# Largest magnitudes across the partitions: a transpose, a vector maximum and a small matmul in place of GpSimd's partition reduce

## The chip, the cores and the metric

The kernel runs on one core of one Trainium2 chip. Its metric is the device time of one execution in microseconds (us). The engines are named as the profile names them: PE is TensorE's matmul, PEld its weight load, DVE is VectorE, ACT is ScalarE, POOL is GpSimd, SP is SyncE, whose queue issues nearly all DMAs here.

## The reference

Eight batches, each of eight heads, with 512 tokens and 32 state rows of 64 values. Every head does an attention both ways between its tokens and its state; the two results are joined, and a feed-forward layer with layer norm and a residual follows.

```python
scores = scale * x @ state.T ;  a = softmax(scores) ;  xread = a @ state
scores2 = scale * state @ x.T ; a2 = softmax(scores2) ; sread = a2 @ x
y = concat([xread, sread], axis=2)        # 8 batches x 544 rows x 512 after joining the heads
xn = (y - mean) / sqrt(var + 1e-6) * g_ln
out = y + max(xn @ w_ch1, 0) @ w_ch2      # 512 -> 2048 -> 512
```

The inputs are float32, the two weights arrive as float64 words.

## The kernel before

TensorE multiplies in float16. Each operand is split in two float16 halves (a rounded value and its remainder), and a product takes three of the four terms. For that, every operand is first scaled by a power of two, which is taken from its largest magnitude. The largest magnitude is needed on every partition alike: first DVE and ACT find it within each partition, and then `partition_all_reduce` on POOL takes the maximum over the 128 partitions and writes it to all of them. This happens in 16 places:

- once for each of the eight batches, in `attention(b)`: `am` (tile x_am, two columns, one for x and one for the state) goes through the reduce in L172 into tile x_m; L173 and `scales` (L130 to L132) make x_s and x_i of it, and then L180, L181, L188 and L189 make the float16 halves of state and x, which DMAs transpose for the scores (L203);
- once for each of the four units of both weights, in `weight_scale` (L413), from tile w_am to w_m; L415 to L419 make the scale w_s of it.

A unit of a weight goes through `convert`: two raw pieces of 1 MB come in by DMA (L460, L507), ACT takes signs (L437, tile sgn) and magnitudes (L405), DVE their maximum and the float32 bits (L406 to L408), then comes the scale, ACT scales (L443), POOL gives the sign back (L444), ACT rounds to float16 (L451), and POOL makes the remainder (L452).

The first batch is computed while the weights come in. `PLAN` gives the order in which the generators of attention of batches 0 and 1 (a0, a1), the units of the first weight (w0 to w3) and of the second (v0 to v3), and the two products of batch 0 (m: L541, evicted by L544 and L545; n: L602, evicted by L654) are traced. From there the tile framework's planner orders the instructions of each engine, by its own model of their durations, and sets all waits; each engine then runs its queue in order. Batch 1 takes the plain first product too (L541), while `weight_sums` (L480 to L487) makes the other pieces of the first weight. Batches 2 to 7 and the state's rows take the first product by Strassen's scheme in seven products a unit (L560), on four accumulators p1 to p4, which ACT and DVE read (L568 to L594, with one addition on POOL, L586), and the second product in L602, evicted by L619. The attention of batch b+1 is traced between the products of batch b, and its layer norm ends in `normalise` (L322 to L372, the power on POOL in L327), whose pieces go through a transposing DMA into tile xnT.

PSUM has eight banks: `ps_f` gives six single banks to `accumulator()` and `ps_a` one pair to `banks()`. The float32 identity `idf` lies in a buffer of the tag "quad" and is read once, for `fold`.

Of the kernel before, what the change touches and what calls it, by code (L numbers as in the profile page):

```python
# [8 lines left out]
F32 = mybir.dt.float32  # L9
# [3 lines left out]
U32 = mybir.dt.uint32  # L13
# [6 lines left out]
TINY = 1e-30  # L20
F64_MIN = 2.0**-15     # the upper word, read as a float32, of the float64 2**-127
F64_AMAX = 2.0**-12    # the same of 2**-103
SX = 2.0**14   # x and state are scaled so that their largest magnitude lies in [SX, 2 SX)
SE = 2.0**12   # softmax numerators in (0, 1] are scaled by this
SN = 4.0       # normalised activations
SG = 2.0**-1
SW1 = 2.0**3
SW2 = 2.0**13

# Operands are split in two float16 halves, and a product takes three of the four terms.  # L30
A_PIECE = (0, 5, 4, 1, 6, 2, 3)   # where the weight's pieces lie, in the order of the products
# The order of the work on the first batch: attention of batches 0 and 1, the two weights by units,
# the two products.
PLAN = (("a0", 8), ("w0", 3), ("a0", 1), ("w1", 5), ("a0", 5), ("v0", 2), ("w1", 3), ("w2", 2), ("w0", 1),
# [13 lines left out]
def moe_attention(ctx: ExitStack, tc: tile.TileContext, x, state, g_ln, w1, w2, out):  # L48
    """The first product of the feed-forward layer goes by Strassen's scheme in Winograd's form:
    the weight in quarters A (features x inputs), the activations in quarters B (inputs x tokens),  # L50
    seven products of their sums and differences."""
    nc = tc.nc
# [4 lines left out]
    P = 128  # L57
    C = S // P           # token chunks of a batch
    G = H // 4           # groups of four heads
    U = DF // 512        # units of four feature tiles, two of each half  # L60
    QK = 1.0 / float(D) ** 0.5
# [3 lines left out]
    small = ctx.enter_context(tc.tile_pool(name="small", bufs=2))  # L65
    ps_f = ctx.enter_context(tc.tile_pool(name="ps_f", bufs=6, space=PSUM))
    ps_a = ctx.enter_context(tc.tile_pool(name="ps_a", bufs=1, space=PSUM))

    def block(kb, tag, bufs, name):
        """kb kilobytes per partition, out of the buffers that go by that tag."""  # L70
        return main.tile([P, kb * 256], F32, name=name, tag=tag, bufs=bufs)
# [27 lines left out]

    # ---- loads that come first  # L100
    def load_batch(b):
# [15 lines left out]

    idf = quad("idf")[:, 0:P]
    make_identity(nc, idf)
# [5 lines left out]
    def scales(m, c, name):  # L125
        """m [P, n], the same on every partition -> with e the power of two at or below each,
        e / c and c / e."""
        n = m.shape[1]
        inv, s = column(small, name + "_i", n), column(small, name + "_s", n)
        nc.vector.tensor_scalar(inv.bitcast(I32), m.bitcast(I32), EXP_MASK, None, ALU.bitwise_and)  # L130
        nc.vector.tensor_scalar(inv, inv, 1.0 / c, None, ALU.mult)
        nc.vector.reciprocal(s, inv)  # L132
        return s, inv

    def absmax(a, t):
        nc.vector.tensor_reduce(a, t, AX.X, ALU.max, apply_absolute_value=True)

    # ---- gain, the same on every partition
    isg = column(main, "isg")
# [6 lines left out]

    # ---- state operands of a batch
    sh = main.tile([P, G, 2, 2, D], F16, name="sh")
# [5 lines left out]
    def attention(b):  # L154
# [16 lines left out]
        m = column(small, "x_m", 2)  # L171
        nc.gpsimd.partition_all_reduce(m, am, P, bass_isa.ReduceOp.max)  # L172
        nc.vector.tensor_scalar_max(m, m, TINY)  # L173
        sc, isc = scales(m, SX, "x")
# [3 lines left out]
        yield  # L178
        # halves of x and of the state side by side, and transposed: (half, d) on the partitions
        nc.scalar.activation(sh[:, :, 0], sj.unsqueeze(2).broadcast_to([P, G, 2, D]), AF.Copy, scale=sst)  # L180
# [16 lines left out]
        yield  # L197
        # scores, (head, state row) on the partitions
        ps = banks()
# [17 lines left out]
        yield  # L217
        # softmax over the tokens: the state's read
        eb = halves("eb").rearrange("p (i g t) -> p i g t", i=2, g=G)
# [9 lines left out]
        yield  # L229
        # softmax over the state rows  # L230
        ts3 = ts.rearrange("p (k n) -> p k n", n=32)
# [38 lines left out]
        if b > 0:  # L270
            # every head's halves of the numerators, twice, down the partitions
            ek = rows("ek").bitcast(F16).rearrange("p (g j t) -> p g j t", g=G, j=4)
            for i in range(2):
                for j in range(4):
                    nc.sync.dma_start(out=ek[32 * i:32 * i + 32, :, j], in_=ea[32 * j:32 * j + 32, i])  # L275
            nc.sync.dma_start(out=ek[64:128], in_=ek[0:64])
# [16 lines left out]
        else:  # L293
            # nothing else is on the tensor engine yet: a bank for every fourth head
            for j in range(4):
# [18 lines left out]
    def normalise(xr, cw, plain):  # L314
        """Layer norm of two halves of cw chunks of rows; the quarters and their sums in halves,
        transposed."""
        w = cw * 256
# [73 lines left out]

    # ---- weights
    def narrow(u, name):
# [6 lines left out]
    def magnitudes(raw, t, most):  # L400
        """float64 words [P, n, 2] -> in t [P, n] float32 of the same magnitude but of either sign,
        and the largest of the upper words read as float32, whose order is that of the float64."""
        ti = t.bitcast(U32)
        low = raw[:, :, 0].bitcast(U32)
        nc.scalar.activation(t, raw[:, :, 1].bitcast(F32), AF.Abs)  # L405
        nc.vector.tensor_scalar(t, t, F64_MIN, F64_AMAX, ALU.max, ALU.max, accum_out=most)  # L406
        nc.vector.tensor_scalar(ti, ti, 7 << 27, 3, ALU.bitwise_xor, ALU.logical_shift_left)
        nc.vector.scalar_tensor_tensor(ti, low, 29, ti, ALU.logical_shift_right, ALU.bitwise_or)  # L408

    def weight_scale(most, c, name):  # L410
        """Largest upper words [P, 2] -> scales, the same on every partition."""
        m = column(small, name + "_m", 2)
        nc.gpsimd.partition_all_reduce(m, most, P, bass_isa.ReduceOp.max)  # L413
        mi = m.bitcast(U32)
        nc.vector.tensor_scalar(mi, mi, 1 << 27, 4, ALU.bitwise_xor, ALU.logical_shift_left)  # L415
        nc.vector.tensor_scalar(mi, mi, 1, EXP_MASK, ALU.logical_shift_right, ALU.bitwise_and)
        inv, s = column(small, name + "_i"), column(small, name + "_s")
        nc.vector.tensor_scalar(inv, m[:, 0:1], m[:, 1:2], 1.0 / c, ALU.max, ALU.mult)
        nc.vector.reciprocal(s, inv)  # L419
        return s, inv  # L420
# [4 lines left out]
    def convert(u, src, spaces, ts, scale, back, target, engine):  # L425
        """Unit u of a weight, as two times [P, 1024] float64 words, in halves of float16."""
        am = column(small, "w_am", 2)
# [27 lines left out]
    def weights1(u):  # L455
        def src(fh, raw):
            f0 = 2 * (fh * (DF // 2) + u * 256)
            # the first unit's words go ahead of the transposes that the scores wait for, the others not
            with tc.issue_after(marks[0].ins) if u > 0 else nullcontext():
                nc.sync.dma_start(out=raw.rearrange("p (k f) -> p k f", k=4),  # L460
                                  in_=w1[:, f0:f0 + 512].rearrange("(k p) f -> p k f", p=P))
# [11 lines left out]
    def weight_sums(u):  # L473
        """The other four pieces of the first weight, from the halves of its quarters."""
        w = w1c[u].rearrange("p m i k f -> p m i (k f)")
# [45 lines left out]
    def common_scale():  # L521
        """The units of the second weight scaled alike, so that one accumulation takes them all."""
        nc.vector.tensor_reduce(uo, uoq, AX.X, ALU.max)
# [7 lines left out]

    # ---- feed-forward layer
    def first_product_plain(u, xT, cw, hids):
        """Unit u of the hidden layer from the quarters themselves."""
        w = cw * P
# [14 lines left out]
    def first_product(u, xT, cw, hids):  # L550
        """Unit u of the hidden layer, two halves of 128 cw tokens, by Strassen's scheme."""
        w = cw * P
# [89 lines left out]

    # ---- the first batch, while the weights come in
    def first_products():
# [15 lines left out]
    for u in range(U):  # L660
        gens[f"w{u}"] = weights1(u)
        gens[f"v{u}"] = weights2(u, spaces[u])
    # each engine's newest instruction of the first attention: the weights' work keeps behind it
    newest = {}
# [59 lines left out]
```

## Time and profile before

| | us |
|---|---|
| median of 3 runs | 898.94 |
| lowest and highest run | 895.89, 899.03 |
| span of the profiled execution | 896.3 |
| PE busy | 739.4 (82%) |
| DVE busy | 520.0 (58%) |
| ACT busy | 328.9 (37%) |
| POOL busy | 216.7 (24%) |

The profile is of one execution. Its span goes from the first to the last instruction; the page gives no other time for that execution, and its span lies 2.6 us below the median of the runs. Engines work side by side, so their busy times add to more than the span, and a busy time says nothing of when an engine was needed. The idle time in front of a group of instructions, and what ended it, says who waited for whom. Ends of matmuls are modelled, and the spans of POOL's own instructions are rough.

### The profile page before, as it was taken

The page shows a single profiled execution, that of the slowest core. Times are in us where ns is not written, and L with a number is a line of the kernel's source. Part 1 is how long each engine was busy: PE and PEld are TensorE (multiplying, and loading weights), DVE is VectorE, ACT ScalarE, POOL GpSimd, SP SyncE. Part 2 cuts the span into 40 slices and gives each one's busy share as a digit, 9 for nine tenths or more (in the row PEclk, how much of TensorE's full clock was granted, in tenths as well). Part 3 has the DMA queues.
Part 4 walks back from the last instruction along what each step waited for, and adds up shares of the span by engine and source line. Part 5 has one row for each costly group of instructions (what it writes and reads, how often), then busy time and mean ns, then how long its engine had stood idle before and what let it go on. Part 6 is the DMA issues. An engine that isn't in the chain of part 4 may idle for free.

```text
span 896.3 us, 12756 instructions
## 1 busy us (share of the span) xinstructions
PE 739.4 (82%) x5136; PEld 447.1 (50%) x5136; DVE 520.0 (58%) x881; ACT 328.9 (37%) x534; POOL 216.7 (24%) x153
## 2 busy tenths in 40 slices
PE   0120535789699799999999999999999999899997
PEld 0020212334234346864785487458745764685493
DVE  5857336847856546755584578357836674472050
ACT  4555343442434324423542354144415342251030
POOL 0147124641838411112011212021201121020010
PEclk9999957988989899999999999999999999999999
DMA  9950515133050238033802551264145322602000
GB/s 221 308 154 0 141 31 119 24 99 104 11 122 18 52 105 158 5 74 88 157 15 61 129 116 24 75 134 87 30 123 116 48 49 61 118 2 42 24 26 23
DMA packets 146586, 73.83 MB, mean 82 GB/s; under 512 B 125472, under 2 KB 137248, under 8 KB 146080
## 3 DMA queue, kind: packets, MB, share of 16 engines
q1 hardware_dynamic: 146384, 72.77, 34.9%
q8 instruction: 40, 0.66, 0.3%
q10 hardware_dynamic: 144, 0.26, 0.1%
q14 instruction: 18, 0.15, 0.1%
HBM read 28.57 MB, written 9.44 MB: 42 GB/s over the span
## 4 chain that ended last, share of the span: by engine, by line
PE 39%; DVE 17%; issue 13%; DMA 11%; POOL 9%; ACT 8%; SPq 3%; DVEq 0%; ACTq 0%; POOLq 0%
PE acc L560 20%; PE acc L602 17%; DMA xnT<-pc 4%; DMA x_f<-in_x_dram 3%; POOL w_t L444 3%; DVE pc L372 2%; POOL sums L480 2%; DMA s_r<-in_state_dram 1%; SPq L275 1%; POOL w2h L452 1%; POOL w1c L452 1%; DVE pc L348 1%; DVE tq L365 1%; ACT x L188 1%; DVE hid L569 1%
## 5 line engine op out<-in xcount | busy, mean ns | idle before, releaser
L602 PE MATMUL acc<-w2h,hid 128*128 128x512 f16 x1632 | 370.4, 386 | 35.6 <-ACT hid L544 15.1
L602 PEld LDWEIGHTS <-hid 128*128 128x128 f16 x1632 | 160.1, 99 | 229.8 <-issue 18.4
L560 PE MATMUL acc<-xnT,w1c 128*128 128x256 f16 (+1 forms) x2352 | 243.7, 265 | 8.9 <-DMA xnT<-pc 7.2
L560 PEld LDWEIGHTS <-w1c 128*128 128x128 f16 x2352 | 214.7, 98 | 39.9 <-issue 11.2
L541 PE MATMUL acc<-xnT,w1c 128*128 128x512 f16 x384 | 93.6, 407 | 46.3 <-DMA xnT<-pc 46.3
L541 PEld LDWEIGHTS <-w1c 128*128 128x128 f16 x384 | 39.7, 104 | 98.0 <-issue 43.7
L586 POOL TENSOR_TENSOR m<-u,m 128x512 f32<-128x512 f32 (+1 forms) x28 | 33.4, 1191 | 205.3 <-DVE u L585 196.0
L322 DVE BATCH_NORM_STATS2 s<-xr 128x6 f32<-128x512 f32 x32 | 20.6, 685 | 64.5 <-ACT xr L291 64.5
L291 ACT ACTIVATE xr<-banks,ux 128x1024 f32<-128x1024 f32 x14 | 15.6, 1114 | 108.5 <-PE banks L289 107.4
L327 POOL TENSOR_TENSOR rs<-rs,mhalf 128x4 f32<-128x4 f32 (+1 forms) x9 | 12.7, 1407 | 171.4 <-DVE rs L326 144.7
L568 ACT ACTIVATE hid<-u 128x512 f16<-128x512 f32 (+1 forms) x56 | 33.2, 594 | 50.9 <-DVE u L589 50.5
L619 DVE SCALAR_TENSOR_TENSOR xr<-acc,uo,xr 128x512 f32<-128x512 f32 x28 | 20.9, 745 | 51.6 <-PE acc L602 51.3
L444 POOL TENSOR_TENSOR w_t<-w_t,sgn 128x1024 f32<-128x1024 f32 x16 | 35.8, 2255 | 40.8 <-issue 21.8
L569 DVE SCALAR_TENSOR_TENSOR hid<-u,hid 128x512 f16<-128x512 f32 (+1 forms) x56 | 41.9, 750 | 0.0
L372 DVE TENSOR_TENSOR pc<-xn,pc 128x512 f16<-128x512 f32 (+1 forms) x28 | 23.5, 877 | 28.9 <-ACT pc L371 28.9
L569 DVE SCALAR_TENSOR_TENSOR hid<-acc,hid 128x512 f16<-128x512 f32 (+1 forms) x28 | 18.1, 648 | 31.8 <-ACT hid L568 31.7
L248 PE MATMUL banks<-ebT,x 128*128 128x64 f16 x256 | 10.3, 205 | 25.8 <-ACT w_t L443 16.8
L443 ACT ACTIVATE w_t<-w_t,w_s 128x1024 f32<-128x1024 f32 x16 | 17.5, 1140 | 38.5 <-DVE w_s L419 22.8
L203 PE MATMUL banks<-xT,sT 128*32 128x512 f16 x128 | 12.0, 428 | 22.2 <-DMA xT<-x 22.2
L568 ACT ACTIVATE hid<-m 128x512 f16<-128x512 f32 (+1 forms) x28 | 16.6, 593 | 36.1 <-POOL m L586 36.1
L573 ACT ACTIVATE m<-acc 128x512 f32<-128x512 f32 (+1 forms) x28 | 15.5, 552 | 38.3 <-PE acc L560 38.3
L371 ACT ACTIVATE pc<-xn 128x512 f16<-128x512 f32 (+1 forms) x28 | 15.1, 588 | 36.9 <-DMA xnT<-pc 36.8
(120 smaller groups left out, 869.9 us busy)
## 6 DMA issues: line engine op xcount, KB each, us to landing
raw<-in_moe_w_ch_dram SPq DMA_DIRECT2D x16, 1024.0 KB, 5.7
x_f<-in_x_dram SPq DMA_DIRECT2D x16, 512.0 KB, 5.8
out_dram<-xr SPq DMA_DIRECT2D x16, 512.0 KB, 3.2
ek<-ea SPq DMA_DIRECT2D x56, 64.0 KB, 2.0
ek<-ek SPq DMA_DIRECT2D x7, 512.0 KB, 4.2
s_r<-in_state_dram SPq DMA_DIRECT2D x32, 64.0 KB, 5.0
s_j<-in_state_dram SPq DMA_DIRECT2D x8, 64.0 KB, 3.1
sread_rows<-sread SPq DMA_DIRECT2D x32, 16.0 KB, 3.1
```

Of the source, the lines that this page charges most:

```text
L322: nc.vector.bn_stats(s6, xr[t][:, c])
L372: nc.vector.tensor_tensor(pc[:, q, 1], v, pc[:, q, 0], ALU.subtract)
L444: nc.gpsimd.tensor_tensor(t, t, sgn[:, fh], ALU.mult)
L452: engine.tensor_tensor(lo, t, hi, ALU.subtract)
L480: nc.gpsimd.tensor_tensor(o, a, b, ALU.add)
L541: nc.tensor.matmul(ps, lhsT=w1c[u][:, q // 2 * 2 + k // 2, i, k % 2, q % 2 * P:(q % 2 + 1) * P], rhs=xT[:, k // 2 * 2:k // 2 * 2 + 2, j, k ...
L560: nc.tensor.matmul(ps[:, f * w:(f + 1) * w], lhsT=w1c[u][:, A_PIECE[m], i, k, f * P:(f + 1) * P], rhs=xT[:, m, j, k * w:(k + 1) * w], star ...
L568: nc.scalar.activation(hi, v, AF.Relu)
L569: nc.vector.scalar_tensor_tensor(lo, v, 0.0, hi, ALU.max, ALU.subtract)
L586: nc.gpsimd.tensor_tensor(m5, u3, m5, ALU.add)
L602: nc.tensor.matmul(po, lhsT=hid[:, i, q, c * P:(c + 1) * P], rhs=w2h[u][:, j, q], start=first and q == 0 and n == 0, stop=last and q == 3 ...
L619: nc.vector.scalar_tensor_tensor(v, po, uo, v, ALU.mult, ALU.add)
```

## The change

The partition reduce on POOL is replaced in both places by a new function `across`. It transposes the columns of largest magnitudes (two columns on 128 partitions) on PE into PSUM, so that each becomes a row on one partition; DVE takes the maximum of each row (2x128); and a second matmul, with that maximum repeated 128 times as its weight and a corner of the identity as its moving operand, writes the two maxima to all 128 partitions. DVE's next instruction reads them from PSUM. The bank for this comes from a new pool `ps_x`, and `ps_f` has five banks in place of six. The identity gets a tile of its own, since it is now needed throughout. The diff also takes out comments, which are left out here.

```diff
-from concourse import bass_isa, mybir
+from concourse import mybir
...
-    ps_f = ctx.enter_context(tc.tile_pool(name="ps_f", bufs=6, space=PSUM))
+    ps_f = ctx.enter_context(tc.tile_pool(name="ps_f", bufs=5, space=PSUM))
     ps_a = ctx.enter_context(tc.tile_pool(name="ps_a", bufs=1, space=PSUM))
+    ps_x = ctx.enter_context(tc.tile_pool(name="ps_x", bufs=1, space=PSUM))
...
-    idf = quad("idf")[:, 0:P]
+    idf = main.tile([P, P], F32, name="idf")
     make_identity(nc, idf)
...
+    def across(a, name):
+        n = a.shape[1]
+        ps = ps_x.tile([P, 512], F32, name="spread")
+        nc.tensor.transpose(ps[0:n, 0:P], a, idf)
+        top = column(small, name + "_t")
+        nc.vector.tensor_reduce(top[0:n], ps[0:n, 0:P], AX.X, ALU.max)
+        nc.tensor.matmul(ps[:, P:P + n], lhsT=top[0:n].broadcast_to([n, P]), rhs=idf[0:n, 0:n], start=True, stop=True)
+        return ps[:, P:P + n]
...
         m = column(small, "x_m", 2)
-        nc.gpsimd.partition_all_reduce(m, am, P, bass_isa.ReduceOp.max)
-        nc.vector.tensor_scalar_max(m, m, TINY)
+        nc.vector.tensor_scalar_max(m, across(am, "x"), TINY)
...
         m = column(small, name + "_m", 2)
-        nc.gpsimd.partition_all_reduce(m, most, P, bass_isa.ReduceOp.max)
         mi = m.bitcast(U32)
-        nc.vector.tensor_scalar(mi, mi, 1 << 27, 4, ALU.bitwise_xor, ALU.logical_shift_left)
+        nc.vector.tensor_scalar(mi, across(most, name).bitcast(U32), 1 << 27, 4, ALU.bitwise_xor, ALU.logical_shift_left)
```

## The prediction

> **What bounds the kernel now.** I read the page's first two parts, then the same span cut by stage, then the chain of work that ended last, then GpSimd's instructions in order of time, and last the waits.
>
> Page, parts 1 and 2: busy time of three engines, then tenths of 40 slices (22.4 us each).
> ```profile
> span 896.3 us, 12756 instructions
> PE 739.4 (82%) x5136; PEld 447.1 (50%) x5136; DVE 520.0 (58%) x881; ACT 328.9 (37%) x534; POOL 216.7 (24%) x153
> PE   0120535789699799999999999999999999899997
> PEclk9999957988989899999999999999999999999999
> ```
> 82% is an average over two unlike stages: from slice 15 on PE is full at full clock, before it PE is half empty and its clock is down. The same by stage (columns: stretch, its length, busy PE, PEld, DVE, ACT, POOL with instructions, granted clock, DMA share, GB/s):
> ```profile
> 0.00:95.00 95.00, 10.39 (x152) 8.36 (x153) 64.75 (x122) 48.83 (x63) 31.50 (x25) 1.00 0.61 168
> 95.00:260.00 165.00, 115.90 (x515) 48.45 (x515) 97.59 (x158) 61.85 (x85) 69.25 (x41) 0.82 0.30 79
> 260.00:328.00 68.00, 62.00 (x347) 29.35 (x346) 41.35 (x69) 25.19 (x43) 31.85 (x23) 0.95 0.22 44
> 328.00:755.00 427.00, 416.96 (x3093) 274.20 (x3091) 262.77 (x440) 160.36 (x275) 69.47 (x50) 1.00 0.40 85
> ```
> After 328 us, PE is busy 416.96 of 427 us: nothing but PE work counts there. Before 328 us no engine is full: in 95 to 260 PE has 115.9 of 165 us, DVE 97.6, POOL 69.3. That stage is a chain of hand-offs, and the chain that ended last says which (start, us, what):
> ```profile
> 65.08 3.54 issue
> ...
> 91.19 1.93 issue
> 93.12 0.37 POOL w_m L413
> 93.50 0.07 POOLq L452 x2
> 93.57 7.03 issue
> 100.60 2.12 POOL w2h L452
> ...
> 253.00 5.73 issue
> ```
> "issue" is time in which an engine waited for nothing the profile shows. POOLq is POOL's sequencer. Each long piece stands directly before a partition reduce (L413, L172) or before the first ordinary POOL instruction after one. POOL's own order of time shows the same, with the idle time before each in brackets:
> ```profile
> 93.12 0.37 POOL L413 PARTITION_ALL_REDUCE w_m<-w_am  x1 [5.82 <-issue]
> 100.60 2.12 POOL L452 TENSOR_TENSOR w2h<-w_t,w2h 128x1024 f16<-128x1024 f32 x1 [7.10 <-issue]
> ...
> 161.18 4.20 POOL L444 TENSOR_TENSOR w_t<-w_t,sgn 128x1024 f32<-128x1024 f32 x2
> 165.35 2.11 POOL L452 TENSOR_TENSOR w2h<-w_t,w2h 128x1024 f16<-128x1024 f32 x1
> ...
> 346.95 0.37 POOL L172 PARTITION_ALL_REDUCE x_m<-x_am  x1 [7.11 <-DVE x_am L136]
> ```
> A reduce takes 0.37 us, but POOL stands about 6 us before it and about 7 us after it. Rows without a bracket, as at 161.18 and 165.35, had no idle time worth a mark: two different lines, no gap. I read the gaps as a change of GpSimd's code, in and out, around the reduce alone. Meanwhile others stand too, among them PE, through ACT:
> ```profile
> DVE w_m L415 <- POOL w_m L413: 25.7, 6, 9.1
> DVE x_m L173 <- POOL x_m L172: 24.2, 4, 16.8
> PE acc L602 <- ACT hid L544: 15.1, 1, 15.1
> ```
> (us in total, times, longest.) The eviction L544 of batch 0 sat in ACT's queue behind scalings (L443, L451) that sat behind POOL.
>
> **The change part by part.** *Removed: 16 reduces and the code changes around them.* Up to 328 us the chain holds ten pieces of this kind (the first is that at 65.08, the last that at 253.00): 3.54 + 1.93 + 7.03 + 5.75 + 4.04 + 5.79 + 5.69 + 6.17 + 5.05 + 5.73 = 50.7 us. If nothing else is late, that goes. After 328 us POOL has 69.5 us of work in 427; the five reduces there find their code change covered by POOL's idle time (7.11 us before the one at 346.95, named as a wait for DVE), and their way back is covered until the next L586, with one exception:
> ```profile
> 695.92 2.09 issue
> ```
> There, ahead of one L586 of the last batch, 2.1 us are saved.
>
> *Added per maximum:* a float32 transpose of two columns, which moves 128 columns of the identity; a DVE maximum over 2x128 out of PSUM; a float32 matmul that moves two columns; and DVE's next step now reads PSUM. Nearest rows:
> ```profile
> L258 PE MATMUL banks<-fold,z 128*128 128x64 f32 x40 | 5.0, 268 | 0.0
> 10.60 0.28 DVE L136 TENSOR_REDUCE x_am<-s_j 128x1 f32<-128x128 f32 x1
> ...
> 515.87 13.70 PE L560 MATMUL acc<-xnT,w1c 128*128 128x256 f16 x124 [0.74 <-DMA xnT<-pc]
> 517.52 0.15 DVE L136 TENSOR_REDUCE x_am<-x_part 128x1 f32<-128x4 f32 x1
> 517.81 0.37 POOL L172 PARTITION_ALL_REDUCE x_m<-x_am  x1 [7.13 <-DVE x_am L136]
> 518.25 0.16 DVE L173 TENSOR_SCALAR x_m<-x_m 128x2 f32<-128x2 f32 x1
> ```
> L258 is 5.0/40 = 0.125 us of PE for 64 float32 columns; 128 columns make 0.25, the spread at most 0.125: 0.375 us of PE. The DVE maximum is 0.28. Three hand-offs of about 0.15 us (x_am ends at 517.67, the reduce starts at 517.81) make the new path 0.375 + 0.28 + 0.45 = 1.1 us from x_am to the scale, where the old one took 518.25 - 517.67 = 0.58. So +0.5 us each; eleven before 328 us (eight for weights, three for x): +5.5 us. After it, five for x: their 0.5 us of latency lies beside PE's products, but PE itself pays 5 x 0.375 = +1.9 us.
>
> *What is queued behind the new waits.* PE works in order, so a transpose whose x_am or w_am is not there holds every product behind it, and the spread holds PE again for DVE's 0.28 plus two hand-offs (0.6 us), unless other matmuls were put between. Bounds in the full stage: from 0 (both find their inputs ready) to about 3 us a batch (at 515.87 the products of a batch begin, x_am ends at 517.67, plus the 1.1 us path), 15 us for five. The order is chosen by a planner that takes what it believes to be ready, and the scores (L203) already go between products at no cost:
> ```profile
> L203 PE MATMUL banks<-xT,sT 128*32 128x512 f16 x80 | 7.2, 384 | 0.0
> L560 PE MATMUL acc<-xnT,w1c 128*128 128x256 f16 x1680 | 187.4, 273 | 6.6 <-DMA xnT<-pc 4.9 <-ACT m L573 1.6
> ```
> I am nearest to that row and take 0.3 us a batch, +1.5. DVE's maximum waits for PE in turn; behind it stand L576 and L569 in the full stage. DVE has 427 - 262.8 us free there: nothing.
>
> *One PSUM bank less for accumulators (6 to 5).* A unit of seven products holds four at once. The wait for an accumulator's reader is 1.6 us in 1680 matmuls (row above). Bounds: 0, and one DVE eviction (0.7 us) at each of 24 units, 17 us. The first accumulator of a unit is read out three products before its end, so I take +1.
>
> *Identity in a tile of its own, the scale read from PSUM:* one buffer of the other tag comes free early; DVE ops of the same 0.16 us. Nothing.
>
> **The sum.** Is the start free to shrink by 50.7 - 5.5 = 45 us, or is another engine next? PE in 95 to 328 has 49.1 + 6.0 = 55 us of idle time, and at full clock its 115.9 us would be 95: room for 75. DVE to 260 us has 64.8 + 97.6 = 162 us of work: busy 85% of the time (my estimate of what fixed queues allow) it would be through by 191, which is room for 69. Both exceed 45, so the chain's figure stands. It is also no more than what batch 0's own path suggests:
> ```profile
> 52.53 4.23 PE L301 MATMUL acc<-sh,ea 32*128 32x64 f16 x88 [1.48 <-DVE ea L268]
> 72.85 1.66 DVE L308 TENSOR_SCALAR xr<-acc,ux 128x256 f32<-128x256 f32 x4 [5.96 <-POOL w_t L444]
> 95.15 12.76 PE L541 MATMUL acc<-xnT,w1c 128*128 128x512 f16 x48 [38.38 <-DMA xnT<-pc]
> ```
> Batch 0's read is done at 56.8, but its second half is copied at 72.85, when POOL frees a buffer (signs, L444) after two code changes. Without them the copy can go at about 58; I put PE's first product at 84 instead of 95, since DVE's weight work fills part of that gap. So 45 us at the start, plus about 2 for buffers that come free earlier: 47. Sum: 896.3 - 47 - 2.1 + 1.9 + 1.5 + 1 = 851.6. The page gives the span of the profiled execution and no time around it; the median of the runs, 898.94, is 2.6 above that span, so I add 2.6: 854.
>
> The clock: it is 0.82 where PE has holes and 1.00 where it has none. "TensorE: Matmul & The Clock Gate" of the Trainium skill (section "What's actually happening") says that the array runs at half rate after an idle window and at full rate after a busy one; the trace agrees in direction (0.82 against 1.00). By that rule closing holes would also return clock, up to 21 us, towards 833; I leave that in the range's low end, since the room comes from the rows above.
>
> **The rivals.** (1) *Another engine takes over half of it.* ACT's and DVE's queues are fixed before the run, so a weight's step that waits can stand before attention's or before an eviction. Then half of 47 stays: 877. For it: DVE has 68% of the first 95 us already; against: 59% in 95 to 260, with the waits on the reduce in it.
> (2) *More comes back*, with the clock: the room is 75, not 45: about 828.
> (3) *Slower: PE's queue is held at the transposes.* Place: the start, where a weight's transpose stands ahead of products, and DMA or DVE brings w_am late. Such holds exist (15.1 us above). To end over 903 the 16 maxima must cost 47 + 4 more, 3.2 us each on PE's path, after 1.1 us of path. Against it: until 95 us PE has only 10.4 us of work. Time if it is 3.5 each: 908.
> (4) *The gap is not the reduce's.* If POOL stands at those places for another reason, nothing goes: 899. Against it: the rows at 161.18 and 165.35, no gap where no reduce is between.
> (5) *The reduce itself was the cheaper way*, its code change being covered: 16 x 0.5 + 1.9 + 1.5 + 1 = +12, 911. Against it: DVE waits 25.7 and 24.2 us for the two reduces. The "GPSIMD Engine Reference" of the Trainium skill (section "Engine selection") says so: a reduce along partitions belongs on GPSIMD and not on VectorE; no run here shows the two beside each other yet.
>
> **How the numbers follow.** Likeliest, 836 to 868: 0.62. Rival 1, 868 to 890: 0.19. Rival 2, below 836: 0.09. Rivals 3 and 5: 0.06. Rival 4: 0.04. Half a per cent (4.5 us) is about what a measurement tells from no change. Faster 0.90, same 0.04, slower 0.06. The range leaves out the ends of rivals 1 and 2 and all of 3 to 5: 824 to 882.
>
> **What would show it.** Right: no idle of 6 to 7 us on POOL before or after a scale; DVE L173 and L415 wait under 2 us; PE's first product near 84 and the stage after 328 starting near 281; clock in the start above 0.82; the full stage, 85.4 us a batch, within 1 us. Wrong: PE waiting on w_am or x_am at a transpose for over 2 us several times; DVE at 90% through the start while PE has holes; or batches in the full stage growing by 2 us or more.

## The result, and the profile after

| | before | changed |
|---|---|---|
| median, us | 897.41 (4 runs) | 863.75 (861.36 to 864.78, 4 runs) |
| span of the profiled execution, us | 896.3 | 861.5 |
| ratio to before, 95% interval | | 0.9623 [0.960, 0.9647] |

The changed kernel is 3.8% faster. The forecast was 854 (824 to 882), so the time lies in the range and 10 us above the forecast. Lines of code moved by 10 to 12 with the change: L203, L408, L444, L452, L541, L560, L586, L602 are now L214, L419, L454, L462, L551, L570, L596, L612; the transpose is L141, DVE's maximum L143, the spread L144.

Page of the changed kernel, parts 1 and 2:
```profile
span 861.5 us, 12789 instructions
PE 742.0 (86%) x5184; PEld 453.2 (53%) x5184; DVE 543.6 (63%) x897; ACT 331.3 (38%) x534; POOL 215.0 (25%) x137
...
PE   0230998964999899999989899989998999999997
...
PEclk9999999976999999999999999999999999999999
```
PE is full from the fifth slice on, with one hole in slices 9 and 10. The same by stage (columns as in the prediction):
```profile
0.00:95.00 95.00, 24.47 (x201) 15.04 (x202) 77.36 (x138) 54.09 (x72) 37.93 (x23) 1.00 0.68 194
95.00:260.00 165.00, 138.69 (x696) 61.90 (x693) 136.05 (x201) 78.88 (x117) 93.39 (x55) 0.93 0.30 75
...
328.00:755.00 427.00, 413.41 (x3025) 271.01 (x3023) 260.88 (x431) 156.51 (x265) 67.30 (x46) 0.99 0.37 79
```
In 95 to 260 us PE rose from 115.9 to 138.7 us with more matmuls (696 for 515) and its clock from 0.82 to 0.93; DVE rose from 97.6 to 136.1 of 165 us. In the stretch from 328 to 755 us PE was busy 3.5 us less. POOL's order of time in the start, idle time in brackets:
```profile
116.12 4.22 POOL L454 TENSOR_TENSOR w_t<-w_t,sgn 128x1024 f32<-128x1024 f32 x2 [3.47 <-ACT w_t L453]
120.29 4.23 POOL L462 TENSOR_TENSOR w2h<-w_t,w2h 128x1024 f16<-128x1024 f32 x2
139.73 4.22 POOL L454 TENSOR_TENSOR w_t<-w_t,sgn 128x1024 f32<-128x1024 f32 x2 [15.21 <-ACT w_t L453]
```
Past the first microsecond no gap of POOL is put down to "issue" any more; POOL waits for others. To see where the 34.8 us of span come from, I take three marks in PE's order: batch 1's first product, the first Strassen product (batch 2), and the first product of the state's rows. Before (first fence) and changed:
```profile
248.63 28.36 PE L541 MATMUL acc<-xnT,w1c 128*128 128x512 f16 x120 [7.92 <-DMA xnT<-pc]
...
346.19 4.09 PE L560 MATMUL acc<-xnT,w1c 128*128 128x256 f16 x36
...
851.84 18.92 PE L560 MATMUL acc<-xnT,w1c 128*128 128x128 f16 x336
```
```profile
206.70 17.18 PE L551 MATMUL acc<-xnT,w1c 128*128 128x512 f16 x72 [13.28 <-DMA xnT<-pc]
...
302.36 5.50 PE L570 MATMUL acc<-xnT,w1c 128*128 128x256 f16 x36 [3.43 <-DMA xnT<-pc]
...
817.03 18.92 PE L570 MATMUL acc<-xnT,w1c 128*128 128x128 f16 x336
```
The start, up to the first Strassen product, gained 346.19 - 302.36 = 43.8 us. The full stage lost: 817.03 - 302.36 = 514.7 us, where it took 851.84 - 346.19 = 505.7, so 9.0 us went back. 43.8 - 9.0 = 34.8 is the whole difference of the spans; what follows the state's rows takes the same time in both.

### The profile page after: what moved, and what is told of

Its sections match the earlier page's. It is cut to its first block, busy times and chain, and to the rows that moved or that the text cites. A ratio compares the mean times of both kernels' runs of the same rounds, so it can differ in the third digit from the quotient of the medians.

```text
span 861.5 us, 12789 instructions
## 1 busy us (share of the span) xinstructions
PE 742.0 (86%) x5184; PEld 453.2 (53%) x5184; DVE 543.6 (63%) x897; ACT 331.3 (38%) x534; POOL 215.0 (25%) x137
## 4 chain that ended last, share of the span: by engine, by line
PE 54%; DVE 20%; DMA 14%; issue 4%; ACT 3%; SPq 3%; POOL 2%; DVEq 0%; ACTq 0%
PE acc L570 24%; PE acc L612 23%; DMA xnT<-pc 5%; PE acc L551 4%; DMA raw<-in_moe_w_ch_dram 3%; DVE pc L383 2%; DVE w_t L419 2%; DMA s_r<-in_state_dram 2%; DVE pc L359 2%; DMA ebT<-eb 2%; DVE x L200 1%; DVE w_t L417 1%; DVE xm L348 1%; DMA x_f<-in_x_dram 1%; SPq L343 1%
## 5 line engine op out<-in xcount | busy, mean ns | idle before, releaser
L612 PE MATMUL acc<-w2h,hid 128*128 128x512 f16 x1632 | 364.4, 382 | 8.5 <-ACT w2h L461 4.1
L570 PE MATMUL acc<-xnT,w1c 128*128 128x256 f16 (+1 forms) x2352 | 250.2, 268 | 14.3 <-DMA xnT<-pc 13.2
L612 PEld LDWEIGHTS <-hid 128*128 128x128 f16 x1632 | 159.2, 99 | 196.3 <-issue 11.7
L570 PEld LDWEIGHTS <-w1c 128*128 128x128 f16 x2352 | 216.6, 99 | 48.1 <-issue 17.6
L551 PE MATMUL acc<-xnT,w1c 128*128 128x512 f16 x384 | 90.4, 391 | 16.8 <-DMA xnT<-pc 16.5
L596 POOL TENSOR_TENSOR m<-u,m 128x512 f32<-128x512 f32 (+1 forms) x28 | 33.4, 1194 | 234.1 <-DVE u L595 174.2
L551 PEld LDWEIGHTS <-w1c 128*128 128x128 f16 x384 | 37.8, 100 | 64.9 <-issue 24.7
L338 POOL TENSOR_TENSOR rs<-rs,mhalf 128x4 f32<-128x4 f32 (+1 forms) x9 | 12.3, 1367 | 169.7 <-DVE rs L337 120.7
L454 POOL TENSOR_TENSOR w_t<-w_t,sgn 128x1024 f32<-128x1024 f32 x16 | 36.4, 2300 | 62.3 <-ACT w_t L453 62.3
L579 DVE SCALAR_TENSOR_TENSOR hid<-u,hid 128x512 f16<-128x512 f32 (+1 forms) x56 | 38.9, 707 | 2.1 <-ACT hid L578 2.1
L583 ACT ACTIVATE m<-acc 128x512 f32<-128x512 f32 (+1 forms) x28 | 15.6, 556 | 54.6 <-PE acc L570 40.9
L245 POOL TENSOR_TENSOR ts<-ts,mA 128x1024 f32<-128x1024 f32 x8 | 16.1, 2008 | 54.9 <-DVE mA L244 53.1
L589 ACT ACTIVATE m<-acc 128x512 f32<-128x512 f32 (+1 forms) x28 | 15.8, 566 | 33.7 <-PE acc L570 24.1
L348 DVE SCALAR_TENSOR_TENSOR xm<-xr,mv,gx 128x512 f32<-128x512 f32 x32 | 28.7, 917 | 0.0
L554 ACT ACTIVATE hid<-acc 128x512 f16<-128x512 f32 x32 | 18.7, 592 | 22.7 <-PE acc L551 22.7
```

The source lines that it names most:

```text
L348: nc.vector.scalar_tensor_tensor(xm, xr[t][:, c], mv[:, n, 0:1], gx, ALU.subtract, ALU.mult)
L454: nc.gpsimd.tensor_tensor(t, t, sgn[:, fh], ALU.mult)
L551: nc.tensor.matmul(ps, lhsT=w1c[u][:, q // 2 * 2 + k // 2, i, k % 2, q % 2 * P:(q % 2 + 1) * P], rhs=xT[:, k // 2 * 2:k // 2 * 2 + 2, j, k ...
L554: nc.scalar.activation(hid[:, 0, q], ps, AF.Relu)
L570: nc.tensor.matmul(ps[:, f * w:(f + 1) * w], lhsT=w1c[u][:, A_PIECE[m], i, k, f * P:(f + 1) * P], rhs=xT[:, m, j, k * w:(k + 1) * w], star ...
L579: nc.vector.scalar_tensor_tensor(lo, v, 0.0, hi, ALU.max, ALU.subtract)
```

## The experiments

The theory after the result: what cost the time before was the change of GpSimd's code around each reduce, whoever reads its result; and the 9 us of the full stage come from where the transpose stands in PE's queue. The rivals: the wait for the reduce's result, the order that the planner makes, the missing accumulator bank.

"Change of code" is my name for it. The trace of the kernel before names something at these places: POOL's sequencer executes two instructions MODIFY_POOL_CONFIG when POOL goes from ordinary instructions to a reduce, and two when it goes back (a pair at 87.49 us, ahead of the reduce at 93.12, and a pair at 93.45, ahead of L452 at 100.60).
```profile
L413 POOLq MODIFY_POOL_CONFIG  x14: 1/12/23, 30.2 to 201.4; - x14
```
(Line, engine, name and count; least, median and longest in ns; first and last start.) The kernel before has 62 of them in all, the changed kernel 2, both at its beginning. They take under 0.1 us each; what passes in the microseconds behind them no row shows, so a change of code stays a reading.

Every kernel was timed against the kernel before (medians of 895.4 to 897.4 us).

**One bank less, nothing else** (the kernel before)

```diff
-    ps_f = ctx.enter_context(tc.tile_pool(name="ps_f", bufs=6, space=PSUM))
+    ps_f = ctx.enter_context(tc.tile_pool(name="ps_f", bufs=5, space=PSUM))
```


> The kernel before with five accumulator banks in place of six; the reduces stay on GpSimd. Theory (the bank costs next to nothing): 0 to +1.5 us against before, batches in the full stage 85.1 us apart as before. Rival (the missing bank is what made the full stage of the changed kernel 9 us longer): +6 to +10 us, with every second batch near 90 us.

896.22 us, ratio 0.9994 [0.998, 1.0009]. The bank costs nothing that can be measured, and it is not what lengthened the full stage: that takes 503.8 us here (505.7 before).

**The old reduce beside the new path, its result unread** (the changed kernel)

```diff
         n = a.shape[1]
+        idle = column(small, name + "_idle", n)
+        nc.gpsimd.partition_all_reduce(idle, a, P, bass_isa.ReduceOp.max)
         ps = ps_x.tile([P, 512], F32, name="spread")
```


> The changed kernel, and at each of its 16 places GpSimd also does the old partition reduce, into a column that nobody reads. Theory (the change of GpSimd's code around each reduce is what cost the time, whoever reads the result): POOL again stands 6 us before and 7 us after each reduce, the start gets 25 to 45 us longer, 890 to 910 us. Rival (what cost was that DVE had to wait for the reduce's result, or the planner's order): 864 to 870 us.

914.26 us, ratio 1.0188 [1.0165, 1.0211]: slower than the kernel before, and more than the theory's 890 to 910. POOL, and PE's first Strassen product:
```profile
94.90 0.37 POOL L141 PARTITION_ALL_REDUCE w_idle<-w_am  x1 [5.77 <-issue]
102.32 2.12 POOL L464 TENSOR_TENSOR w2h<-w_t,w2h 128x1024 f16<-128x1024 f32 x1 [7.05 <-issue]
```
```profile
351.17 4.09 PE L572 MATMUL acc<-xnT,w1c 128*128 128x256 f16 x36 [3.48 <-DMA xnT<-pc]
```
The gaps are back, 5.77 and 7.05 us, though nobody waits for the reduce's result. MODIFY_POOL_CONFIG is back too, 58 times. The start is 351.17 - 302.36 = 48.8 us longer than the changed kernel's. So the idle time around the reduce costs by itself; the wait for its result is not needed for it.

The planner's order as a rival is answered in part. Up to ACT's last copy L317 of batch 0, at 56.3 us in the changed kernel, the order of every engine is the same in both, apart from the reduces and the new path's own instructions, and here that copy comes at 68.6 us: 12.3 us late with no change of order. From there on ACT, then DVE, PE and POOL, have some instructions in another order. The chain that ended last up to the first Strassen product holds six idle pieces around reduces, 5.95 + 7.47 + 4.57 + 7.38 + 7.72 + 5.66 = 38.8 us; how much of the other 10 us is order, no run tells.

Against the kernel before, which has the same gaps, the start is 351.17 - 346.19 = 5.0 us longer. That is the new path, with the planner's new order in it and with the waits for the reduce's result taken away: a net figure, not the path alone.

**GpSimd's reduce again where its code change is covered** (the changed kernel, batches 3 to 7)

```diff
-        nc.vector.tensor_scalar_max(m, across(am, "x"), TINY)
+        if b > 2:
+            nc.gpsimd.partition_all_reduce(m, am, P, bass_isa.ReduceOp.max)
+            nc.vector.tensor_scalar_max(m, m, TINY)
+        else:
+            nc.vector.tensor_scalar_max(m, across(am, "x"), TINY)
```


> The changed kernel, but batches 3 to 7 (those of the full stage) take x's and the state's magnitudes by GpSimd's reduce again; weights and batches 0 to 2 stay with the transpose. Theory (the start's gain is the code changes taken away, and the full stage loses because the transpose stands late in PE's queue): first Strassen product still near 302 us, batches 85 us apart, 854 to 857 us. Rival (the loss in the full stage is the bank or comes from another shift of order): 862 to 865 us.

854.3 us, ratio 0.9524 [0.9501, 0.9546].
```profile
301.68 24.10 PE L574 MATMUL acc<-xnT,w1c 128*128 128x256 f16 x204 [3.48 <-DMA xnT<-pc]
...
806.19 18.92 PE L574 MATMUL acc<-xnT,w1c 128*128 128x128 f16 x336
```
The start stays (301.68), and the full stage takes 504.5 us, as before the change. So its 9 us do come from doing the maxima of these five batches by the transpose. That could still be the path's own length or its place.

**The transpose early in PE's queue** (the changed kernel)

```diff
-                if plain or (u + n) % 2 == 0:
+                if plain or (u + n) % 2 == 0 and (u > 1 or (u, n) == (1, 5)):
                     next(work, None)
+                elif u == 0 and n < 3:
+                    steps(work, 2)
```


> The changed kernel with the attention's first six steps traced between the first three products of a batch (two steps after each) and none until the sixth product of the second unit, so that the planner may put the transpose at most three products after the batch's start; nothing else differs. Theory (the transpose's late place, 13.5 us after the start in every second batch, shifts the attention and makes PE wait for xnT): transposes within 5 us of the start in all batches, batches within 1 us of 85.1, 854 to 859 us. Rival (it is the 1.1 us path itself or the bank): 862 to 866 us.

852.91 us, ratio 0.9505 [0.9485, 0.9525]. In the changed kernel, the second Strassen batch (DVE's x_am, then PE from the batch's first product to the next batch's):
```profile
388.47 0.15 DVE L148 TENSOR_REDUCE x_am<-x_part 128x1 f32<-128x4 f32 x1
```
```profile
387.17 4.09 PE L570 MATMUL acc<-xnT,w1c 128*128 128x256 f16 x36 [0.15 <-DMA xnT<-pc]
...
400.90 0.27 PE L141 MATMUL spread<-idf,x_am 128*2 128x128 f32 x1
...
434.94 1.84 PE L259 MATMUL banks<-ebT,x 128*128 128x64 f16 x32 [2.22 <-DMA ebT<-eb]
...
458.43 0.63 PE L300 MATMUL banks<-sk,ek 128*128 128x64 f16 x16
458.89 15.92 PE L612 MATMUL acc<-w2h,hid 128*128 128x512 f16 x73
478.32 5.76 PE L570 MATMUL acc<-xnT,w1c 128*128 128x256 f16 x36 [3.50 <-DMA xnT<-pc]
```
and in this kernel:
```profile
301.61 5.76 PE L570 MATMUL acc<-xnT,w1c 128*128 128x256 f16 x36 [3.42 <-DMA xnT<-pc]
...
386.84 4.09 PE L570 MATMUL acc<-xnT,w1c 128*128 128x256 f16 x36
390.77 0.27 PE L141 MATMUL spread<-idf,x_am 128*2 128x128 f32 x1
391.42 2.67 PE L570 MATMUL acc<-xnT,w1c 128*128 128x256 f16 x23 [0.38 <-DMA xnT<-pc]
...
470.65 4.09 PE L570 MATMUL acc<-xnT,w1c 128*128 128x256 f16 x36
...
807.39 18.92 PE L570 MATMUL acc<-xnT,w1c 128*128 128x128 f16 x336
```
In the changed kernel x_am was there at 388.6 and the transpose came at 400.9, 12.3 us later and behind 120 products: not because anything was late, but because the planner had put it there. In the fourth batch it came 14.4 us after x_am, in the other three 3.5 to 4.0. The attention moved back with it. PE waits 2.22 us for ebT, and after the attention's last matmuls (458.43) only 73 products are left to cover the layer norm and its DMA; PE waits 3.50 us for xnT. That batch took 478.32 - 387.17 = 91.2 us, and the fourth the same way 89.5 (652.55 - 563.05); the others 84.7 to 84.9. With the transposes early the same batch takes 83.8 us, and the full stage 807.39 - 301.61 = 505.8. That is 1.3 us more than with GpSimd's reduce in batches 3 to 7 (504.5), some tenths of a microsecond a batch. The trial moves the attention's other first steps forward too, and GpSimd's reduce was not run with that order, so the price of the path by itself is not told apart from the order.

**Only the weights by the transpose** (the changed kernel, `across(am, "x")` replaced by GpSimd's reduce in all eight batches)

> The changed kernel with the eight reduces of the attention (x and the state) back on GpSimd, the eight of the weights by the transpose. Theory (each code change in the start counts with its own piece of the chain, and those of the full stage are covered): against the kernel that gives back only batches 3 to 7 (854.3), batches 1 and 2 bring two code changes back into the start, 6 to 13 us: 860 to 867 us. Rival (only the weights' reduces matter, the attention's are covered everywhere): 853 to 856 us.

863.48 us, ratio 0.9646 [0.9632, 0.9661]; 9.2 above the kernel that gives back batches 3 to 7 only. Batch 1's first product, the first Strassen product, and POOL's rows around batch 2's reduce:
```profile
216.82 15.00 PE L552 MATMUL acc<-xnT,w1c 128*128 128x512 f16 x60 [9.04 <-DMA xnT<-pc]
...
313.03 4.09 PE L571 MATMUL acc<-xnT,w1c 128*128 128x256 f16 x36
```
```profile
226.90 0.37 POOL L184 PARTITION_ALL_REDUCE x_m<-x_am  x1 [5.83 <-issue]
234.52 1.14 POOL L491 TENSOR_TENSOR sums<-w1c 128x512 f32<-128x512 f16 x1 [7.25 <-DVE x_am L148]
```
Batch 1's first product is at 216.82, against 206.2 there, so 10.6 us are lost before it, where the reduces of batches 0 and 1 stand (with the planner's order changed in places). Batch 2's reduce has the same gaps, 5.83 and 7.25 us, but from batch 1's first product to the first Strassen product it takes 313.03 - 216.82 = 96.2 us, against 301.68 - 206.23 = 95.5 there: 0.8 us for it. So what a reduce costs depends on what else the start waits for, even where its gaps are as long.

**What the start waits for next: DVE's queue?** PE's longest wait in the changed start is 13.28 us for batch 1's xnT. Ahead of that layer norm DVE rescales the second weight (L540). Two trials, both on the kernel with early transposes. The first traces the rescaling later:

```diff
             if plain:
                 weight_sums(u)
+        if plain:
+            common_scale()
...
-    common_scale()
```


> The kernel with the attention's first steps traced early (852.9), and the rescaling of the second weight's halves (four passes of 1.2 to 2.5 us on DVE) traced after the first product of batch 1 in place of before it. Theory (DVE's queue is what the start waits for next: the rescaling stands there ahead of batch 1's layer norm, and PE waits 12.4 us for its xnT): first product of batch 1 at 197 to 200 us in place of 205.7, and 845 to 849 us. Rival (something else holds batch 1, or the rescaling returns the time later): 851 to 855 us.

855.2 us, ratio 0.9567 [0.954, 0.9594]. It tells nothing: the planner left the passes where they were (three at 180.72, batch 1 at 205.61). The second binds them with an ordering edge: `marks["pc"]` holds the latest remainder (L359) of a layer norm in `normalise`, and when the rescaling is traced that is the last one of batch 1.

```diff
-                    nc.vector.scalar_tensor_tensor(lo, xm[:, a], rs[:, n:n + 1], hi, ALU.mult, ALU.subtract)
+                    marks["pc"] = nc.vector.scalar_tensor_tensor(lo, xm[:, a], rs[:, n:n + 1], hi, ALU.mult, ALU.subtract)
...
+            with tc.issue_after(marks["pc"].ins):
-            nc.vector.tensor_scalar(v, v, ratio[:, u:u + 1], None, ALU.mult)
+                nc.vector.tensor_scalar(v, v, ratio[:, u:u + 1], None, ALU.mult)
```


> As the kernel with the attention's first steps traced early (852.9), and the four rescaling passes of the second weight (L540 there, 7.4 us for three of them) are kept in DVE's queue behind the last remainder of batch 1's layer norm by an ordering edge; in the trial before, the planner had put them at the same place whatever the trace order. Theory (DVE's queue is what the start waits for next): first product of batch 1 at 196 to 200 us in place of 205.7 and 845 to 849 us. Rival (the passes return the time inside batch 1, which has DVE work for the weights' sums): first product early, but 851 to 856 us.

852.2 us, ratio 0.9511 [0.9478, 0.9543], not to be told from the 0.9505 without it. DVE and PE in this kernel:
```profile
183.57 2.51 DVE L348 SCALAR_TENSOR_TENSOR xm<-xr,mv,gx 128x512 f32<-128x512 f32 x1
...
198.30 3.67 DVE L541 TENSOR_SCALAR w2h<-w2h,ratio 128x4096 f16<-128x4096 f16 x3
```
```profile
202.49 17.10 PE L552 MATMUL acc<-xnT,w1c 128*128 128x512 f16 x72 [7.61 <-DMA xnT<-pc]
...
300.69 5.76 PE L571 MATMUL acc<-xnT,w1c 128*128 128x256 f16 x36 [4.75 <-DMA xnT<-pc]
```
Batch 1 starts 3.2 us earlier (202.49 for 205.65), not the 6 to 10 expected, and batch 2 only 0.9 (300.69 for 301.61). The rival holds in the main: most of the little that is gained is given back inside batch 1.

**DVE's instructions beside POOL.** The rows of the two trials show one more thing: three passes of the rescaling took 3.67 us at 198 in the second trial, and 7.40 us at 181 in the first, where POOL was at work. Over the start, the changed kernel's DVE was busy for 229.9 us up to 296 us, while the kernel before needed 211.0 up to 340; the maxima explain 11 x 0.27 = 3 of the 19. The trial moves the remainders L462 from POOL to DVE (`nc.gpsimd` to `nc.vector` as the engine of `convert` in `weights1` and `weights2`):

> As the kernel with the attention's first steps traced early (852.9), and the remainders of the converted weights (L462, 16 passes of 128x1024, 2.1 to 2.8 us each on POOL) go to DVE. In the start of the changed kernel the same DVE instructions take longer than before the change: L419 1.63 us on average where it (as L408) took 1.22, L348 1.21 against 0.89, the rescaling L540 2.44 against 1.51. Theory (DVE's instructions are stretched while POOL runs): with half of POOL's weight work gone L419 falls below 1.4, L348 below 1.0 and L540 below 1.8, and DVE's busy time to 296 us (230) rises by less than the 16 x 1.2 = 19 us of the new passes; time 845 to 862 us, since DVE is the next engine. Rival (the stretch comes from elsewhere, such as PE's or ACT's denser work): the three means stay, DVE's busy time rises by 19 us or more, 858 to 870 us.

858.01 us, ratio 0.9556 [0.9535, 0.9577]. DVE's groups in the start, before, changed, and in this trial:
```profile
L408 DVE SCALAR_TENSOR_TENSOR w_t<-raw,w_t 128x1024 uint32<-128x1024 uint32 x16 | 19.5, 1220 | 0.1
L530 DVE TENSOR_SCALAR w2h<-w2h,ratio 128x4096 f16<-128x4096 f16 x4 | 5.9, 1508 | 0.0
```
```profile
L419 DVE SCALAR_TENSOR_TENSOR w_t<-raw,w_t 128x1024 uint32<-128x1024 uint32 x16 | 26.1, 1633 | 0.1
L540 DVE TENSOR_SCALAR w2h<-w2h,ratio 128x4096 f16<-128x4096 f16 x4 | 9.6, 2436 | 0.0
```
```profile
L419 DVE SCALAR_TENSOR_TENSOR w_t<-raw,w_t 128x1024 uint32<-128x1024 uint32 x16 | 21.2, 1328 | 0.0
L540 DVE TENSOR_SCALAR w2h<-w2h,ratio 128x4096 f16<-128x4096 f16 x4 | 5.4, 1394 | 0.0
```
With half of POOL's weight work gone, L419 and L540 fall most of the way back, and DVE's busy time to 296 us is 227.5 us although it took over 16 passes worth 23 us (12.7 + 10.5). Its start is 4.7 us longer; up to the first Strassen product DVE is busy for 233.1 us (to 306.3), against 231.8 (to 301.6) without the trial, so 23 us of passes came in and its sum rose by 1.3. L348 stayed at 1.16 (1.21), against the theory's number; POOL's L454 still runs beside it. So in the start DVE's instructions are stretched beside POOL's, and giving POOL's work to DVE still costs 5 us.

## Why the prediction was right, step by step

- *The code changes, -50.7 in the start:* right in kind. Putting the reduces back costs 48.8 us, with nothing waiting for the result. The list of pieces is not exact: the chain of the kernel before has one more of the kind, 2.31 us at 42.04, in front of L444, after the first two reduces of the weights. And a piece on the chain was taken for a gain of its own length. For the last one, 5.73 us at 253.00, that fails: from batch 1's first product to the first Strassen product the kernel before takes 346.19 - 248.63 = 97.6 us and the changed one 95.7, so 1.9 us went there, and in the trial with the weights alone by the transpose, which has that reduce again, 0.8 came back. The start gained 43.8 where the sum had 47, which this piece could explain, but no run tells the terms apart that finely.
- *The new path, +5.5 in the start:* the number came out near (+5.0 net), which is partly luck, since the 5.0 hold the planner's order too. The instructions have about the estimated sizes, save that the spread is two matmul instructions and takes 0.38 us where 0.125 was allowed (tile of the new bank, changed kernel; name, count, ns least/median/most, first and last start):
```profile
L144 PE MATMUL spread<-idf,x_t x16: 246/266/370, 11.7 to 661.1; 2*128 2x2 f32 x16
...
L141 PE MATMUL spread<-idf,x_am x8: 272/273/372, 11.0 to 658.1; 128*2 128x128 f32 x8
L143 DVE TENSOR_REDUCE x_t<-spread x8: 269/278/279, 11.4 to 658.5; 2x1 f32<-2x128 f32 x8
```
but the path isn't 1.1 us long: DVE's maximum stands in a fixed queue.
```profile
70.22 0.37 PE L141 MATMUL spread<-idf,w_am 128*2 128x128 f32 x1 [15.25 <-DVE w_t L417]
81.71 0.58 PE L144 MATMUL spread<-idf,w_t 2*128 2x2 f32 x2 [11.12 <-DVE w_t L143]
```
From transpose to spread it is 3.1 us at best for the weights and 11.5 at worst. PE stood at the transposes and spreads too, which the prediction had named as a sign of being wrong: 10.02 and 15.25 us for w_am, and 2.68, 3.06 and 11.12 us for DVE's maximum. All five lie ahead of PE's first product at 85.55, in front of which PE still waited 3.25 us for xnT, so they did not hold the products.
- *2 us more at the start from buffers that come free early:* not seen apart. PE's first product came at 85.55 (84 forecast), and still the start gained 43.8, not 47.
- *PE's own time, 0.375 us a maximum:* right, 0.11 and 0.31 from start to start of the next product (400.90 to 401.01, 403.61 to 403.92), 0.42 in all.
- *PE held at the transposes, +1.5 in the full stage:* this is the term that was mis-sized most. Of the 9.9 us between the forecast span of 851.6 and the measured 861.5, 6.7 lie in the full stage (it lost 9.0, the sum had -2.1 + 1.9 + 1.5 + 1 = 2.3) and 3.2 in the start. I bounded it by a transpose that comes too early and holds PE (0 to 15 us), and took the row where scores go between products at no cost. The opposite happened: it came 12.3 and 14.4 us after its input in two of five batches, and the stage lost 9.0 us, since the attention has no such time to spare. The prediction had named its sign ("batches growing by 2 us or more") but not this mechanism.
- *The bank, +1:* nothing measurable.
- *The piece ahead of L586, -2.1:* not to be told from these runs; with GpSimd's reduces and with early transposes the full stage takes 504.5 and 505.8 us, against 505.7 before.
- *DVE as the next engine:* the room of 69 us reckoned with DVE's work as it was. It is 19 us more in the changed start, 3 of them the maxima, and of the rest the two lines shown above make 10. Whether that cost part of the start, no run tells.
- *The clock:* 0.93 in 95 to 260 us, as holes closed. The rule of the Trainium skill weighed in the prediction ("TensorE: Matmul & The Clock Gate", "What's actually happening") agrees again in direction; the gain that it would add is not seen apart from the rest.
- *Rival 5, the reduce as the cheaper way:* in the full stage, where the code change is covered, GpSimd's reduce (504.5 us) and the early transpose (505.8) are equal within what one profile can tell; in the start the transpose is 43.8 us faster. The "GPSIMD Engine Reference" of the Trainium skill (section "Engine selection") gives reduces along partitions to GPSIMD and not to VectorE; that section does not speak of a way through TensorE, and in the start of this kernel its choice is the slower one by these 43.8 us.

The best version run is the transpose everywhere with the early trace order, 852.9 us (0.9505); holding the rescaling back makes no measurable difference to it, and the kernel with GpSimd's reduce in batches 3 to 7 (0.9524) is not told apart from it.

## What to carry to other kernels

An idle time in front of an instruction that waits for nothing, and again behind it, is a price of the instruction that its own 0.37 us doesn't show; count it on the chain of work, and leave the instruction where the engine is idle anyway. A piece of the chain is not yet a gain of its own length: the start may wait for something else just behind it, as with batch 2's reduce. A short step that moves to a full engine is placed by the planner, so look at how long after its input it runs, not only at its length. Of the two trials with the rescaling, the trace order alone moved nothing, and the ordering edge did.

## What the runs showed of the hardware that I had not expected

- Between POOL's ordinary instructions and its partition reduce lie about 6 us in and 7 us out each time (5.77 and 7.05 with an unread result), not once at first use. Two reduces in a row have no such gap between them: with the unread results, that of x starts at 110.77 us right behind that of a weight (110.48, 0.37 us).
- Some of DVE's instructions took up to two and a half times as long beside POOL's large elementwise instructions: L419 3.03 us at 51.11 us, beside L454, and 1.21 us at 72.75, where POOL had the small L338 (128x4) until L462 began at 73.69. Of the 16 passes of L419 in the changed kernel the four that started while L454 or L462 ran took 2.56 to 3.03 us, the other twelve 1.16 to 1.23. Not every instruction is stretched: L417, on the same tile, took 1.18 to 1.22 us all 16 times, at 68.98 wholly inside L462.
```profile
50.48 7.73 POOL L454 TENSOR_TENSOR w_t<-w_t,sgn 128x1024 f32<-128x1024 f32 x3
51.11 3.03 DVE L419 SCALAR_TENSOR_TENSOR w_t<-raw,w_t 128x1024 uint32<-128x1024 uint32 x1
...
68.38 2.57 POOL L462 TENSOR_TENSOR w2h<-w_t,w2h 128x1024 f16<-128x1024 f32 x1
68.98 1.18 DVE L417 TENSOR_SCALAR_CACHE_REDUCE w_t<-w_t 128x1024 f32<-128x1024 f32 x1
...
72.26 1.45 POOL L338 TENSOR_TENSOR rs<-rs,mhalf 128x4 f32<-128x4 f32 x1 [1.31 <-DVE rs L337]
72.75 1.21 DVE L419 SCALAR_TENSOR_TENSOR w_t<-raw,w_t 128x1024 uint32<-128x1024 uint32 x1
```
POOL pays as well: L462 took 2.5 us on average in the changed start, where the same instruction (L452) took 2.2 before, and when L419 started first, at 153.81, it kept its 1.16 us and POOL's L253, which began at 154.04, took 2.70 (the same line takes 1.91 us elsewhere). With its stalls taken away POOL runs beside DVE more, and DVE's instructions get longer; what that costs of the gain, no run separates.
